# Eight idle bf16 matmuls at the start become five, followed by 64 matmuls on 32x32 tiles of the array

## The chip, the cores and the metric

The kernel runs on one core of one Trainium2 chip. The metric is the device time of one execution in microseconds. Three runs of the kernel before took 342.63, 343.73 and 343.97 us; the median is 343.73 us.

## The reference

The reference is block-causal attention over 8 batches and 8 heads (sequence 576, head size 64, blocks of 64), followed by a soft mixture of experts on its output, all in fp32:

```python
scores = scale * np.matmul(q, k.transpose(0, 1, 3, 2))      # q, k, v: (8, 8, 576, 64)
scores = np.where(block_i >= block_j, scores, -1e9)
attn = softmax(scores);  x = (attn @ v) laid out as (4608, 512)

logits = x @ phi                        # phi: (512, 32), 8 experts of 4 slots
d = softmax(logits, axis=0)             # over all 4608 rows
slot_input = d.T @ x                    # (32, 512)
slot_out[e] = relu(slot_input[e] @ w1[e]) @ w2[e]   # w1, w2: 16 MB each
c = softmax(logits, axis=1)
out = c @ slot_out                      # (4608, 512)
```

Softmax subtracts the maximum and adds 1e-9 to the sum. The matmuls that the change touches compute nothing of this.

## The kernel before

The attention stage goes through 32 pairs of heads. For each pair it loads q, k and v (SP issues the DMAs), scales k on POOL (`scale_k`, line 426), computes the scores on PE (`qk`, line 462, and `qkb`, line 483), finds row maxima on DVE (`rowmax`, lines 496 and 501), takes exponentials on ACT (line 511), normalises on POOL, transposes the probabilities on PE (line 549) and multiplies with v (lines 581 and 591). After each batch of four pairs come the logits (lines 609 and 616) and the running sums of the expert inputs. All these steps of all pairs are put in one list, each with a due time from a table written out by hand, and are emitted sorted by that time (`at`, and the loop at line 859); on each engine they run in that order, and `tc.manual_schedule` leaves the order as it is.

After the attention stage the experts follow: `up` (line 961), `down` (line 981), and the output `emit` (line 936), with the weights arriving by DMA in 32 pieces of 1 MB.

A PSUM tile `ps_all` of 128 partitions by 4096 fp32 columns is all eight banks; `bank` picks 512 columns of it. `idle` is a 128x64 bf16 tile of zeros, set by DVE at line 281. `acc` is a 128x512 fp32 tile, zeroed by POOL at line 289, in which the expert inputs are summed up much later.

Because `warm` is given the due times -50, -49.99 and so on, its matmuls are the first that PE executes. They multiply zeros by zeros: 128 rows by 64 columns of the array, 512 moving columns, into the bank `pb`, and nothing reads the result. PE's first real work comes behind them in its queue: the scores of the first pair, `qk` with "5" (two fp32 calls with 384 columns, one on rows 0 to 63 of the array, one on rows 64 to 127), which need q and the scaled k. DVE's first pass over scores (line 496) needs these.

An fp32 call of `nc.tensor.matmul` appears in the trace as two pairs of a weight load (LDWEIGHTS) and a MATMUL.

`tile_position=(r, c)` puts a matmul on the part of the array that begins at row r and column c; the size of the part is that of its operands. Line 609 uses four parts of 128 rows by 32 columns, line 936 four of 32 rows by 128 columns, line 483 four of 64 by 64.

Of the kernel before, what the change touches and what calls it, by code (L numbers as in the profile page):

```python
# [18 lines left out]
NS = 32  # L19
# [18 lines left out]
NPB = 2  # L38
ONE = "3"
NXT = 6  # L40
WARM = 8
RES = 17

XIN = (2, 3)
# [209 lines left out]
def tile_attention_softmoe(  # L254
# [9 lines left out]
    nc = tc.nc  # L264
# [9 lines left out]
    for qd in range(2):  # L274
        for g in range(4):
            r = slice(NS * g, NS * (g + 1))
# [3 lines left out]
    idle = const.tile([128, 64], BF16, name="idle")  # L280
# [4 lines left out]
    acc = const.tile([128, DM], F32, name="acc")  # L285
# [50 lines left out]
    with ExitStack() as c1:  # L336
# [3 lines left out]
        ps_all = ps.tile([128, 4096], F32, name="ps")  # L340

        def bank(k, i=0, z=""):
            n = BK.get(k + z, BK.get(k))[i]
            return ps_all[:, 512 * n:512 * n + 512]
# [53 lines left out]
        def at(t, fn, *args):  # L398
            ops.append((t, len(ops), fn, args))

        probs, xTs, xps = {}, {}, {}
# [28 lines left out]
        def warm(i):  # L430
            if i == 0:
                xps["w"] = bank("pb", 0, ".0")
            nc.tensor.matmul(  # L433
                xps["w"][0:64], lhsT=idle, rhs=idle[:, 0:64].unsqueeze(1).broadcast_to([128, 8, 64]), start=True, stop=True
            )


        def fill(bank, n):
# [362 lines left out]

        for i in range(WARM):
            at(-50 + 0.01 * i, warm, i)
# [58 lines left out]
    with ExitStack() as c2:  # L862
        start = c2.enter_context(ExitStack())
# [190 lines left out]
```

## Time and profile before

| | |
|---|---|
| median of three runs | 343.73 us (342.63 to 343.97) |
| profiled execution | 344.26 us, its span 342.2 us |
| PE busy | 330.0 us (96%), 5664 matmuls |
| DVE, ACT, POOL busy | 272.6, 257.5, 206.6 us |
| granted clock of PE, mean | 0.988 |

The span goes from the first to the last instruction; the execution's time has some 2 us more around it. Engines are PE (matrix), PEld (its weight loads, which overlap with PE), DVE, ACT, POOL and SP (which issues the DMAs). Times are microseconds from the span's start. A matmul's duration in the trace contains its latency; durations of matmuls side by side overlap, so start times are the better guide to throughput.

### The profile page before, as it was taken

Reading aid. Unit: us, or ns where it says so; the run is one execution under the profiler, and the core shown is the slowest. Engines: PE = TensorE matmul, PEld = TensorE weight load, DVE = VectorE, ACT = ScalarE, POOL = GpSimd, SP = SyncE. Lnnn points to the kernel's source line nnn. Section 1 sums busy time; section 2 is a strip of 40 time slices with the busy share of each in tenths; the row PEclk is TensorE's granted clock in tenths of the full one; section 3 lists DMA queues with packets and bytes.
Section 4 is the critical chain, followed back from the end, with each engine's and each line's share of the span. In section 5 each row is a group of like instructions: output and inputs, shape, how many; then the busy total and the mean of one; then the engine's idle time right before and its main releaser. Section 6 shows DMA issues by size and latency. Waiting matters only on the chain.

```text
span 342.2 us, 14342 instructions
## 1 busy us (share of the span) xinstructions
PE 330.0 (96%) x5664; PEld 231.3 (68%) x5664; DVE 272.6 (80%) x821; ACT 257.5 (75%) x850; POOL 206.6 (60%) x475
## 2 busy tenths in 40 slices
PE   8899999999999999999999999999999998999991
PEld 4567767767866786678667866786677875256660
DVE  5987888899889998998889988988898766373442
ACT  3998999889988898889888988898889823222332
POOL 3888794769577957695769576957777832100000
PEclk9999999999999999999999999999999999899997
DMA  5756629535643585356445863664322299999887
GB/s 180 249 166 215 229 73 318 174 92 208 216 146 98 213 300 179 100 212 212 132 114 214 297 178 92 226 215 157 106 72 71 51 365 402 362 424 406 356 324 306
DMA packets 29938, 72.28 MB, mean 211 GB/s; under 512 B 6960, under 2 KB 15280, under 8 KB 25776
## 3 DMA queue, kind: packets, MB, share of 16 engines
q1 hardware_dynamic: 29872, 71.38, 60.3%
q8 instruction: 44, 0.72, 0.8%
q14 instruction: 22, 0.18, 0.2%
HBM read 61.93 MB, written 9.44 MB: 209 GB/s over the span
## 4 chain that ended last, share of the span: by engine, by line
PE 93%; DVE 4%; issue 1%; DVEq 0%; ACT 0%
PE ps L581 22%; PE ps L549 16%; PE ps L462 15%; PE ps L483 11%; PE ps L591 6%; PE hp L961 5%; PE so L981 4%; PE o L936 3%; PE ps L718 3%; PE ps L609 2%; PE ps L738 2%; DVE ps L496 1%; PE ps L616 1%; PE ps L433 1%; DVE stat L501 1%; PE ps L747 1%
## 5 line engine op out<-in xcount | busy, mean ns | idle before, releaser
L511 ACT ACTIVATE arena<-ps,stat 128x384 f32<-128x384 f32 (+6 forms) x288 | 152.9, 543 | 25.3 <-DVE stat L496 21.9
L529 POOL TENSOR_SCALAR arena<-arena,stat 128x512 f32<-128x512 f32 (+6 forms) x288 | 152.8, 550 | 16.6 <-DVE stat L518 13.1
L496 DVE CUSTOM_DVE_ANT_1 ps<-ps,mask 128x384 f32<-128x384 f32 (+1 forms) x128 | 77.7, 635 | 7.4 <-PE ps L462 6.3
L394 DVE COPY arena<-ps 128x384 f32<-128x384 f32 (+3 forms) x134 | 68.4, 555 | 9.9 <-PE ps L549 3.8
L581 PE MATMUL ps<-arena 128*64 128x256 f32 (+2 forms) x640 | 76.1, 384 | 0.0
L392 ACT COPY arena<-ps 128x384 f32<-128x384 f32 (+3 forms) x142 | 65.2, 495 | 11.0 <-PE ps L549 7.6
L501 DVE TENSOR_REDUCE stat<-ps 128x1 f32<-128x64 f32 (+4 forms) x160 | 57.9, 402 | 6.1 <-ACT arena L511 3.7
L581 PEld LDWEIGHTS ps<-arena 128*64 128x64 f32 x640 | 40.9, 137 | 31.7 <-issue 18.8
L549 PE MATMUL ps<-ident,arena 64*128 64x64 f32 x1600 | 61.0, 226 | 1.0 <-ACT arena L511 0.8
L462 PE MATMUL ps<-arena 64*128 64x384 f32 (+1 forms) x256 | 61.1, 567 | 0.6 <-ACT arena L511 0.6
L549 PEld LDWEIGHTS ps<-ident,arena 64*128 64x128 f32 x1600 | 56.2, 139 | 4.8 <-ACT arena L511 0.9
L511 ACT ACTIVATION_READ_ACCUMULATOR arena<-ps,stat 128x1 f32 x288 | 59.4, 206 | 0.0
L483 PEld LDWEIGHTS ps<-arena 64*64 64x64 f32 x768 | 36.5, 133 | 21.2 <-ACT arena L392 4.6
L522 POOL TENSOR_SCALAR stat<-stat 128x2 f32<-128x2 f32 (+1 forms) x96 | 19.0, 198 | 47.4 <-ACT arena L511 41.4
L483 PE MATMUL ps<-arena 64*64 64x288 f32 (+4 forms) x768 | 42.9, 341 | 0.0
L462 PEld LDWEIGHTS ps<-arena 64*128 64x128 f32 x256 | 24.3, 189 | 10.1 <-DVE arena L394 4.0
L426 POOL TENSOR_SCALAR arena<-arena 128x576 f32<-128x576 f32 x32 | 21.6, 676 | 6.1 <-DMA arena<-in_k 4.6
L591 PE MATMUL ps<-arena 128*64 128x64 f32 x640 | 24.3, 222 | 0.0
L591 PEld LDWEIGHTS ps<-arena 128*64 128x64 f32 x640 | 22.6, 138 | 0.4
L394 DVE COPY xT<-ps 128x512 f32<-128x512 f32 (+1 forms) x27 | 15.2, 580 | 9.1 <-PE ps L581 8.8
L946 DVE COPY arena<-o 128x512 f32<-128x512 f32 (+1 forms) x20 | 11.7, 632 | 13.1 <-PE o L936 13.0
L496 DVE DVE_READ_ACCUMULATOR2_ANT stat<- 128x1 f32 x128 | 17.9, 140 | 0.0
(116 smaller groups left out, 286.2 us busy)
## 6 DMA issues: line engine op xcount, KB each, us to landing
arena<-in_w SPq DMA_DIRECT2D x32, 1024.0 KB, 7.1
arena<-in_k SPq DMA_DIRECT2D x32, 288.0 KB, 3.0
arena<-in_q SPq DMA_DIRECT2D x32, 288.0 KB, 3.2
out<-arena SPq DMA_DIRECT2D x18, 512.0 KB, 4.2
arena<-in_v SPq DMA_DIRECT2D x32, 256.0 KB, 3.4
arena<-in_v SPq DMA_DIRECT2D x32, 32.0 KB, 3.5
arena<-in_phi SPq DMA_DIRECT2D x1, 64.0 KB, 3.9
```

Source lines behind the costliest of these rows:

```text
L392: nc.scalar.copy(out=out, in_=in_)
L394: nc.vector.tensor_copy(out=out, in_=in_)
L426: nc.gpsimd.tensor_scalar(out=area(f"ks{m % NQB}"), in0=area(f"ks{m % NQB}"), scalar1=SCALE, scalar2=0.0, op0=ALU.mult, op1=ALU.add)
L462: nc.tensor.matmul(scores(t + str(j), m), lhsT=q[r, lo:lo + 128], rhs=k[r, 0:NC[t]], start=True, stop=True)
L483: nc.tensor.matmul(o, lhsT=a, rhs=b, start=True, stop=True)
L496: nc.vector.tensor_tensor_reduce(out=sc, in0=sc, in1=ms, scale=-1.0, scalar=-NEG, op0=ALU.add, op1=ALU.min, accum_out=st[:, 0, u:u + 1],)
L501: nc.vector.tensor_reduce(out=st[:, 0, u:u + 1], in_=scores(x, m), axis=AX.XY if x == "8" else AX.X, op=ALU.max, negate=True)
L511: nc.scalar.activation(out=pr, in_=sc, func=AF.Exp, bias=st[:, 0, u:u + 1], accum_out=st[:, 1, u:u + 1], scale=-1.0 if x[0] in "75" else 1.0,)
L529: nc.gpsimd.tensor_scalar(out=pr, in0=pr, scalar1=st[:, 2, u:u + 1], scalar2=0.0, op0=ALU.mult, op1=ALU.add)
L549: nc.tensor.transpose(out=trbank(m, g)[i][:, 64 * n:64 * n + 64], in_=prob(m, x)[r, 128 * c:128 * c + 128], identity=ident[r, r],)
L581: nc.tensor.matmul(xps[m, 0][64 * j:64 * j + 64, lo:hi], lhsT=vs(m)[:, j, c, :], rhs=rhs, start=n == 0, stop=n == 4, skip_group_check=True,)
L591: nc.tensor.matmul(xps[m, 1][64 * j:64 * j + 64, 0:64], lhsT=vs(m)[:, j, c, :], rhs=arena[:, lo:lo + 64], start=(c == 0), stop=(c == NQ - 1),)
```

## The change

`WARM` goes from 8 to 9. Calls 0 to 4 of `warm` stay as they are. Each of the calls 5 to 8 issues 16 matmuls instead: for each of four row groups j and four column groups c of the array, a 32x32 weight tile from `acc`, 128 moving columns from `acc` (rows of group j), with the result in partitions 32c to 32c+31 of the first 128 columns of bank j. `acc` still holds its zeros, and nothing reads the results.

```diff
-WARM = 8
+WARM = 9
...
         def warm(i):
             if i == 0:
                 xps["w"] = bank("pb", 0, ".0")
-            nc.tensor.matmul(
-                xps["w"][0:64], lhsT=idle, rhs=idle[:, 0:64].unsqueeze(1).broadcast_to([128, 8, 64]), start=True, stop=True
-            )
+            if i < 5:
+                nc.tensor.matmul(
+                    xps["w"][0:64], lhsT=idle, rhs=idle[:, 0:64].unsqueeze(1).broadcast_to([128, 8, 64]), start=True, stop=True
+                )
+                return
+            for j in range(4):
+                for c in range(4):
+                    r = slice(NS * j, NS * (j + 1))
+                    nc.tensor.matmul(
+                        ps_all[NS * c:NS * (c + 1), 512 * j:512 * j + 128], lhsT=acc[r, 0:NS], rhs=acc[r, 128:256],
+                        start=True, stop=True, tile_position=(NS * j, NS * c),
+                    )
```

(`NS` is 32.)

## Rows read from the trace of the kernel before

**Rows 1.** The page: span, busy time by engine, instruction queue.
```profile
span 342.2 us, 14342 instructions
PE 330.0 (96%) x5664; PEld 231.3 (68%) x5664; DVE 272.6 (80%) x821; ACT 257.5 (75%) x850; POOL 206.6 (60%) x475
...
PEclk9999999999999999999999999999999999899997
...
q8 instruction: 44, 0.72, 0.8%
```

**Rows 2.** The chain of waits, 0 to 30 us: start, us, what.
```profile
0.95 3.62 PE ps L433 x8
4.57 1.63 PE ps L462 x4
6.21 0.55 DVE ps L496
...
14.59 0.81 DVE arena L394 x2
15.39 0.04 issue
15.44 1.17 PE ps L549 x27
```

**Rows 3.** Busy time by stage: stretch, length, engines (instructions), clock, DMA, GB/s.
```profile
6.20:15.40 9.20, 7.68 (x83) 5.10 (x83) 9.16 (x32) 8.43 (x31) 7.12 (x23) 1.00 0.67 210
15.40:280.00 264.60, 264.56 (x4660) 194.07 (x4662) 231.58 (x708) 229.75 (x776) 194.12 (x438) 1.00 0.54 175
280.00:289.50 9.50, 8.01 (x169) 5.89 (x166) 6.73 (x22) 2.92 (x12) 1.06 (x4) 1.00 0.99 389
289.50:293.10 3.60, 3.60 (x17) 0.79 (x17) 1.54 (x4) 0.68 (x1) 1.16 (x1) 0.53 1.04 376
```

**Rows 4.** Instructions in order of time, 0 to 14 us: start, us, instruction.
```profile
0.87 0.53 POOL L289 MEMSET acc<- 128x512 f32 x1
...
0.95 3.62 PE L433 MATMUL ps<-idle 128*64 128x512 bf16 x8 [0.95 <-DVE zrun L292]
...
3.58 0.67 POOL L426 TENSOR_SCALAR arena<-arena 128x576 f32<-128x576 f32 x1 [1.70 <-DMA arena<-in_k]
...
4.50 0.51 PEld L462 LDWEIGHTS ps<-arena 64*128 64x128 f32 x4 [0.81 <-POOL arena L426]
```

**Rows 5.** Lines 433, 462 (4 to 6.2), 483 (first four; 6 to 7.4): ns min/median/max.
```profile
L433 PE MATMUL ps<-idle x8: 634/634/636, 1.0 to 3.9; 128*64 128x512 bf16 x8
...
L462 PE MATMUL ps<-arena x4: 844/925/1007, 4.5 to 5.3; 64*128 64x384 f32 x4
...
L483 PE MATMUL ps<-arena x4: 451/522/541, 6.1 to 6.1; 64*64 64x288 f32 x2, 64*64 64x256 f32 x1, 64*64 64x192 f32 x1
...
L483 PE MATMUL ps<-arena x24: 216/376/541, 6.1 to 7.3; 64*64 64x288 f32 x8, 64*64 64x256 f32 x4, 64*64 64x192 f32 x4, 64*64 64x128 f32 x4
```

**Rows 6.** PE's matmuls in order of time, 6.05 to 6.12 us.
```profile
5.30 0.85 PE L462 MATMUL ps<-arena 64*128 64x384 f32 x2
6.09 0.55 PE L483 MATMUL ps<-arena 64*64 64x288 f32 x4
```

**Rows 7.** Line 609, 56.4 to 57.7 us: order of time (one narrow window), then durations.
```profile
56.52 0.32 PE L609 MATMUL ps<-xT,arena 128*32 128x128 f32 x4
...
56.52 0.64 PE L609 MATMUL ps<-xT,arena 128*32 128x128 f32 x16
56.98 0.62 PE L609 MATMUL ps<-arena 128*32 128x128 f32 x16
...
L609 PE MATMUL ps<-xT,arena x16: 272/273/297, 56.5 to 56.9; 128*32 128x128 f32 x16
```

**Rows 8.** Line 936, 310.82 to 310.85 us: order of time, then durations.
```profile
310.83 0.71 PE L936 MATMUL o<-cT,s 32*128 32x512 f32 x4
...
L936 PE MATMUL o<-cT,s x4: 692/692/692, 310.8 to 310.8; 32*128 32x512 f32 x4
```

**Rows 9.** The chain of waits, 262 to 343 us: start, us, what.
```profile
263.32 1.01 PE ps L609 x32
264.33 0.45 PE ps L616 x32
...
289.49 3.58 PE hp L961 x16
293.07 0.31 PE z_ps L877 x2
293.38 12.15 PE hp L961 x112
```

## The prediction

> **What bounds the kernel now.** I went from the page to the chain of waits, then to the stages, then to the first microseconds line by line. The page has PE busy 330.0 of 342.2 us [rows 1]; the reader should see that this average hides two stretches without full PE. The chain of the first 30 us shows the first: it goes through the eight idle matmuls (0.95 to 4.57), through the first four score matmuls of line 462 (to 6.20), and then stays on DVE until 15.39, from where PE carries it [rows 2]. The stages say the same by busy time: DVE 9.16 of 9.20 us between 6.20 and 15.40, then PE 264.56 of 264.60 us up to 280 [rows 3]. So whatever makes the first scores late pushes a full DVE, which pushes a full PE, and I take such a delay to reach the end one for one. From 280 on DVE chains, the clock (0.53 granted between 289.5 and 293.1) and PE share the time [rows 3]; all of it follows the attention stage and shifts with it.
>
> The change sits ahead of all this. The idle matmuls are cover for the wait on the first k: POOL starts scaling it at 3.58, when its DMA is in, takes 674 ns (to 4.25), and PE's first score weight load is released by that at 4.50 [rows 4]. Eight idle matmuls of 512 columns start 427 ns apart ((3.62 - 0.634) / 7), that is 1.2 columns per ns, the 1.2 GHz level, and the last has streamed at 0.95 + 8 x 0.427 = 4.37 [rows 4, 5]. They end just as k is ready. The page's clock row shows 9 for these slices; I go by the durations. The clock rises while the first group of line 483 runs: its first four passes take 451 to 541 ns, and later ones of the same shapes are shorter (median 376 over the stage) [rows 5]. I set the rise at 6.3, an estimate between their start at 6.09 and their end.
>
> **The change part by part.**
>
> *Removed:* three idle matmuls, 3 x 0.427 = 1.28 us of PE. Alone this would gain nothing, because the first score load waits for POOL until 4.50 anyway.
>
> *Added:* 64 calls. An fp32 call is two instruction pairs of load and matmul: line 609 has 16 calls to a batch (four chunks by four groups) and 32 matmuls in the trace [rows 9]. So 128 loads and 128 matmuls. A matmul of 128 fp32 columns takes two cycles a column: line 609's first sixteen, four at a time, start at 56.52 and its next sixteen at 56.98, so a step takes (0.46 - 0.025) / 4 = 0.109 us at the 2.4 GHz level (256 cycles; the 0.025 is the first weight load, below) [rows 7]; at 1.2 GHz 256 cycles are 0.213 us.
>
> No row has 32x32 tiles, so how many run at once must be bounded. One at a time costs 128 x 0.213 = 27.3 us at 1.2 GHz; sixteen at once is 8 steps x 0.213 = 1.71 us. The nearest rows each show four tiles side by side: four column tiles (line 609: four starts span 0.32 - 0.297 = 0.02 us, 7 ns apart), four row tiles (line 936: 0.71 us for four of 0.692) and two by two (line 483: 0.55 us for four of up to 0.541) [rows 5 to 8]. Reads of sixteen tiles are four streams to a partition, as in line 609; writes are four row groups to four banks, as in line 936. Both are shown at full speed, so I take sixteen at once. Issue fits: 16 x 7 ns = 0.11 us a step, under 0.213.
>
> The Trainium skill has a rule against this: "TensorE: Matmul & The Clock Gate", in the section "Wait — 56ns, not 53.3ns?", says that matmuls never start closer than about 25 ns. By it the added part would take 128 x 25 ns = 3.2 us. The trace disagrees for tiles beside each other: line 616's 32 matmuls take 0.45 us of the chain, 14 ns each [rows 9].
>
> *The sum.* Five idle matmuls stream until 0.95 + 5 x 0.427 = 3.09. A change of tile form costs 0.14 us: the second passes of line 462 start at 5.30 and stream 384 x 2 / 1.2 = 0.64 us, to 5.94, and the new form starts at 6.09 [rows 6]. So the rounds start at 3.23. The first weight load adds 0.05 (297 against 272 ns in line 609, twice that at half clock [rows 7]), the eight steps 1.71, the staggered starts 15 x 7 ns = 0.10: end 5.09. Another change of form: the first score load starts at 5.23 instead of 4.50. Its first pass waits 0.16 for weights as now (1.007 against 0.844 us [rows 5]), to 5.39; two passes of 0.64 would end at 6.67, but from 6.3 the clock is double, which halves the last 0.37: end 6.48. Now they end at 5.94. **The first scores come 0.53 us late**; the matmuls after them lose nothing, since more of them run at 2.4 GHz.
>
> *What hides in this:* acc, which the new matmuls read, is zeroed by POOL from 0.87 for 0.53 us, long before 3.23 [rows 4]. The banks that they write are PE's own at that time, in order. The 256 instructions are about one more instruction packet (44 packets for some 11,500 PE instructions); such a packet takes 0.8% x 16 x 342.2 / 44 = 1.0 us of a DMA engine [rows 1]. I cost it at nothing, as it is fetched ahead behind the slow idle matmuls; uncovered it is at most 1.0 us.
>
> The profiled execution takes 344.26 us, a 342.2 us span and 2.1 around it, and is 0.53 above the median of the runs. On its own time the sum is 344.26 + 0.53 = 344.79; on the median 343.73 + 0.53 = 344.3. The runs before spread over 1.3 us, more than the effect. Under 0.5% (1.7 us) I count as no change.
>
> **The rivals.**
>
> *A start floor, or eight tiles at once.* With 3.2 us for the rounds they end near 6.5, the scores start at 6.6 and, all at the 2.4 level (0.1 for weights, then 2 x 0.32), end at 7.35: 1.4 late, 345.1. For it: sixteen tiles with two passes each need PE to look past far more waiting instructions than the rows with four show. Against it: the 14 ns of line 616.
>
> *Four at once (slower).* If PE gets no further ahead than in the rows, the rounds are 32 steps: 6.83 us at 1.2 GHz. 3.03 pass before 6.3, the other 3.80 take 1.90; end 8.2, scores start 8.34, end 9.08: 3.1 late, **346.9**. It decides as soon as the scores end 1.7 late, at 7.67: the rounds would then last until 6.8, which by the same arithmetic is about seven tiles at once. For it: nothing beyond four is shown. Against it: row and column tiles each reach four, and line 483 combines them.
>
> *The clock rises sooner.* The idle matmuls use 64 of 128 columns; full-array rounds might bring the 2.4 GHz level earlier. At best it rises at 3.23: the rounds take 8 x 0.11, the scores start at 4.50 behind POOL and end at 5.24 instead of 5.94: 0.7 gained, 343.0. Against it: in the profile PE was busy without a gap from 0.95 and the level still stayed at 1.2 GHz past 6.09, and the first 3 us are unchanged.
>
> *The late clock dip moves.* Line 961's first 16 matmuls take 3.58 us of the chain, where 16 of the next 112 take 12.15 / 7 = 1.74 [rows 9]: 1.84 us for a dip that starts at 289.6, beside a stretch of PE gaps. If the shift moved it off that work, 344.3 - 1.8 = 342.4. That the dip depends on when the program starts is likely, so this is mostly spread, not effect.
>
> **How the numbers follow.** Sixteen at once 0.57 (344.3, own range 343.2 to 345.2), floor or eight 0.15 (345.1), four or fewer 0.12 (346.9 and more), earlier clock 0.10 (343.0), dip moved 0.06 (342.4). The prediction is 344.3. The range 342.9 to 345.9 leaves out the four-at-once case and the moved dip, some 2 in 10. Slower by over 0.5% (above 345.45): four or fewer, a third of the floor case and a tail of the first, 0.20. Faster (below 342.0): only dip and clock together, 0.05. Within: 0.75.
>
> **What would show it.** Line 433 keeps 427 ns for five matmuls. The new line has 128 matmuls, with sixteen starts inside 0.12 us and about 1.9 us in all; the gaps on either side are 0.14. The first load of line 462 starts at about 5.2, the first DVE pass of line 496 at about 6.7 instead of 6.19, and PE takes over the chain at about 15.9 instead of 15.44. Starts of 25 ns or more apart, or steps in groups of four, show the slower rivals; score passes of 0.32 us spacing before 5.5 the earlier clock. The forecast is wrong in kind if the DVE stretch absorbs the delay, so that PE takes over at 15.4 as before.

## The result, and the profile after

The changed kernel took 344.61 us (median of 12 runs, 343.88 to 347.9); the kernel before, in the same series, 343.49 (12 runs, 341.81 to 345.4). The ratio is 1.0052, interval 1.0029 to 1.0075: slower by 1.1 us on the medians, and by 1.8 (1.0 to 2.6) by the ratio, right at the bound of 0.5% between "no change" and "slower". The ratios here and below are formed over the runs of a series and not from the two medians, and leave out one run of e4 that fell in a slower state. The prediction was 344.3 us, range 342.9 to 345.9.

The two profiled executions hardly differ (span 342.1 against 342.2 us), but not because nothing changed: two delays in the one and a clock dip in the other happen to be of like size. First the page of the changed kernel, against [rows 1].

```profile
span 342.1 us, 14592 instructions
...
PE 329.2 (96%) x5789; PEld 232.2 (68%) x5789; DVE 272.6 (80%) x821; ACT 257.5 (75%) x850; POOL 206.6 (60%) x475
...
PEclk9999999999999999999999999999999999999996
```

There are 250 more instructions (256 for the rounds, less three pairs), 45 instruction packets instead of 44, and no 8 in the clock row where the kernel before has one near the end.

Next the changed kernel's first 8 us in order of time (start, us, instruction), against [rows 4, 6]. The change shifts the line numbers: the idle matmuls are line 434, the new rounds 441, the scores 471 and 492 (462 and 483 before), DVE's pass 505 (496).

```profile
0.95 2.34 PE L434 MATMUL ps<-idle 128*64 128x512 bf16 x5 [0.95 <-DVE zrun L292]
3.22 2.59 PE L441 MATMUL ps<-acc 32*32 32x128 f32 x128
5.75 0.92 PE L471 MATMUL ps<-arena 64*128 64x384 f32 x4
6.59 1.32 PE L492 MATMUL ps<-arena 64*64 64x288 f32 x24
...
6.69 0.57 DVE L505 CUSTOM_DVE_ANT_1 ps<-ps,mask 128x384 f32<-128x384 f32 x1 [2.25 <-PE ps L471]
```

The rounds start at 3.22, as computed, but the scores follow at 5.75 and not at 5.23. The scores then need 0.92 us instead of 1.65, because the clock has risen already. The same kernel's chain of waits for the first 30 us shows the net effect, against [rows 2].

```profile
5.82 0.90 PE ps L471 x4
6.71 0.55 DVE ps L505
...
15.94 1.17 PE ps L558 x27
```

DVE starts at 6.71 (6.21 before), PE takes over at 15.94 (15.44 before): 0.50 us late at both. Line 590 (line 581 before) opens one group of matmuls per pair of heads; its groups start 0.49 to 0.53 late for the first 21 pairs, and 1.40 late for the 22nd. What happened between them is in the chain of waits around 196 us, first of the changed kernel:

```profile
193.50 0.91 PE ps L471 x4
...
195.67 0.45 PE ps L625 x32
196.11 0.23 PE ps L727 x2
196.35 0.72 issue
197.06 1.16 PE ps L727 x29
198.22 0.70 PE ps L471 x4
```

and the same place in the kernel before (618, 625 and 727 are 609, 616 and 718 there):

```profile
195.18 0.50 PE ps L616 x32
195.68 1.15 PE ps L718 x30
196.82 0.70 PE ps L462 x4
```

PE stops for 0.72 us in the middle of line 727, with nothing to wait for that the profile shows. I read this as PE having run out of instructions; e3, below, shows such a stop beside the transfer of a packet. The next line starts at 198.22 instead of 196.82, 1.40 late. Another 0.19 is regained before the expert stage, where the chain of the changed kernel reads, against [rows 9]:

```profile
290.70 1.92 PE hp L970 x16
...
292.93 12.15 PE hp L970 x112
```

It begins at 290.70 (289.49 before), 1.21 late, but these sixteen matmuls take 1.92 us instead of 3.58: the profiled execution of before had a clock dip here (0.53 granted from 289.5 to 293.1, [rows 3]), and this one has none. So 1.21 lost minus 1.66 gained leaves line 970's remaining 112 matmuls 0.45 earlier; at the end of the span only 0.1 of this is left. The dip is not an effect of the change: of the full kernels below e3, e9 and e10 show it in their profiles, the others don't.

### The profile page after: what moved, and what is told of

Read it like the earlier page. It is cut to its first block, busy times and chain, and to the rows that moved or that the text cites. A ratio compares the mean times of both kernels' runs of the same rounds, so it can differ in the third digit from the quotient of the medians.

```text
span 342.1 us, 14592 instructions
## 1 busy us (share of the span) xinstructions
PE 329.2 (96%) x5789; PEld 232.2 (68%) x5789; DVE 272.6 (80%) x821; ACT 257.5 (75%) x850; POOL 206.6 (60%) x475
## 4 chain that ended last, share of the span: by engine, by line
PE 94%; DVE 2%; ACT 1%; issue 1%; DVEq 0%
PE ps L590 22%; PE ps L558 17%; PE ps L471 15%; PE ps L492 12%; PE ps L600 6%; PE so L990 4%; PE hp L970 4%; PE o L945 3%; PE ps L727 3%; PE ps L618 2%; PE ps L747 2%; PE ps L625 1%; ACT arena L520 1%; PE ps L441 1%; PE ps L756 1%
## 5 line engine op out<-in xcount | busy, mean ns | idle before, releaser
L471 PE MATMUL ps<-arena 64*128 64x384 f32 (+1 forms) x256 | 60.4, 561 | 0.5 <-ACT arena L520 0.5
```

The costliest lines, as they stand in the source:

```text
L471: nc.tensor.matmul(scores(t + str(j), m), lhsT=q[r, lo:lo + 128], rhs=k[r, 0:NC[t]], start=True, stop=True)
```

## The experiments

Two questions: does the delay of the first scores explain the result, and why did the rounds take longer than computed? Theory A (late scores) is that the first scores' delay alone is what the end sees. Its rivals are that the rounds or their form move the rise of the clock, and, once the hole at 196 us had been seen, theory B (packets): the shifted count of PE's instructions opens holes in the dense part of the attention stage. In the profile's terms, the first rise is the first clock record of a trace; ahead of it durations are at the 1.2 GHz level. Diffs are against the changed kernel unless they say otherwise, and each ratio is to the kernel before, run in the same series.

**e1: the five idle matmuls alone, no rounds.**

```diff
-WARM = 9
+WARM = 5
```

> Five idle matmuls and no 32x32 matmuls at all. Late-scores theory (the loss is the time by which the rounds hold back the first score matmul): idle work ends at 3.09, the first score load starts at 4.50 behind POOL as in the kernel before, the first DVE score pass starts at 6.2; the time is that of the kernel before within 0.2%. Clock rival (the work ahead of the scores sets when the 2.4 GHz level comes): 1.4 us without PE work, so the level comes later than the 5.4 to 6.3 us of the two profiles, the scores and the first line of 64x64 matmuls run at 1.2 GHz, first DVE pass still near 6.2, but PE takes over the chain more than 1 us after 15.4 and the time rises by 1 to 2 us.

Measured: 346.39 us (7 runs) against 343.07; 1.0086 [1.0046, 1.0127]. Its first scores in order of time, and then its chain of waits at 198 us:

```profile
4.56 1.65 PE L471 MATMUL ps<-arena 64*128 64x384 f32 x4 [1.26 <-POOL arena L426]
6.14 2.41 PE L492 MATMUL ps<-arena 64*64 64x288 f32 x24
```
```profile
198.74 0.99 issue
199.74 1.15 PE ps L727 x28
```

The scores start on time, but behind 1.26 us of idle PE the clock rose only at 9.63, line 492 took 2.41 us instead of 1.40, and PE took over at 16.65. So cover of some sort is needed: leaving it out costs at least as much as the change (the two intervals overlap). And the hole is here too, where no rounds ever ran; its count of PE instructions is 6 fewer than before.

**e2: two rounds.**

```diff
-WARM = 9
+WARM = 7
```

> Five idle matmuls and two rounds of 16 instead of four. Late-scores theory: in the profile of the changed kernel a round takes 0.43 us when it is the first and 0.66 us after that at 1.2 GHz, so two end near 4.4 and the first score load starts at 4.5 to 4.7; time that of the kernel before plus 0 to 0.2 us. Rival (any 32x32 round costs a fixed amount, by a change of the array's form): first score load no earlier than 5.2 and most of the changed kernel's loss stays.

Measured: 345.39 against 343.07; 1.0065 [1.0038, 1.0092]. Its chain of waits at two places:

```profile
127.00 0.92 PE ps L727 x24
127.92 0.85 issue
...
309.80 1.11 issue
```

The first scores are no longer late (first matmul at 4.68, DVE at 6.13, PE takes over at 15.39), and still the kernel loses as much. Theory A alone is refuted. With 122 more PE instructions than before, there are holes of 0.85 and 1.11 us, at other places.

**e3: eight rounds.**

```diff
-WARM = 9
+WARM = 13
```

> Five idle matmuls and eight rounds of 16 instead of four. Late-scores theory: four more rounds of 0.41 us (2.4 GHz level) to 0.66 us (1.2) delay the first score load by 1.6 to 2.6 us against the changed kernel's 5.75, to 7.4 to 8.4; the score matmuls then all run at 2.4 GHz, so DVE starts at 8.3 to 9.3, and the time is 2 to 3 us above the kernel before. Rival (the delay is absorbed before PE takes over, and the measured difference is the spread of the clock): time within 0.5 us of the changed kernel's.

Measured: 351.61 (6 runs) against 343.07; 1.024 [1.0194, 1.0287], some 8 us above the kernel before, where I had expected 2 to 3. Its chain of waits, 3 to 10 us:

```profile
3.29 4.31 PE ps L441 x214
7.60 1.55 issue
9.15 0.84 PE ps L441 x34
```

The rounds ran dry for 1.55 us in their own middle, at 7.60, while a packet of the instruction queue was in transfer from 6.75 to 7.70. The clock, up at 6.85, fell at 10.26 behind this stop and rose again at 13.67; PE took over at 21.48. So an uncovered packet cost 1.55 us here, not the "at most 1.0" of the prediction.

**e4: the same rounds in bf16**, one pass instead of two.

```diff
-    lhsT=acc[r, 0:NS], rhs=acc[r, 128:256],
+    lhsT=idle[r, 0:NS], rhs=idle[r, 0:64].unsqueeze(1).broadcast_to([NS, 2, 64]),
```

> Four rounds of 16 as in the change, but on bf16 zeros, so that each call is one load and one matmul instead of two of each. Window theory (the hole between rounds comes from PE holding only so many instructions at a time, about one fp32 round): 32 instructions a round fit twice, so the rounds follow without a hole, 0.11 us each at 1.2 GHz or as fast as instructions are issued (16 pairs at 7 to 9 ns: 0.11 to 0.15), end by 3.9, first score load at 4.50, time that of the kernel before within 0.2%. Rival (each new round of calls waits for the last to drain, whatever its type): a hole of about 0.2 us after each round stays, end near 4.5, first score load at 4.5 to 4.8.

Measured: 345.79 (11 runs) against 343.07; 1.0072 [1.0043, 1.0102]. In order of time:

```profile
3.23 0.85 PE L441 MATMUL ps<-idle 32*32 32x128 bf16 x64
4.53 1.65 PE L471 MATMUL ps<-arena 64*128 64x384 f32 x4 [0.46 <-POOL arena L426]
6.11 2.41 PE L492 MATMUL ps<-arena 64*64 64x288 f32 x24
```

The scores start on time, but with 0.46 us of idle PE ahead of them the clock rose at 8.52, PE took over at 16.37, and there is a hole of 1.11 at 310.4. (At 203.8 PE waits 0.26 us for POOL, behind a k whose DMA took 6.28 us; that is no hole of this kind.) Again no gain from scores that start on time. What this kernel shows of the rounds' own duration is taken up in the next section.

**e5: the count alone, 6 fewer instructions.** The idle time of before in other pieces, no 32x32 tiles: one bf16 idle matmul and two fp32 calls of 448 columns, together as long as eight.

```diff
-WARM = 9
+WARM = 3
...
-            if i < 5:
+            if i == 0:
...
+            else:
+                nc.tensor.matmul(xps["w"][0:64, 0:448], lhsT=acc[:, 0:64], rhs=acc[:, 0:448], start=True, stop=True)
```

> The kernel before with PE's program six instructions shorter and the idle stretch equally long: one bf16 idle matmul and two fp32 ones of 448 columns (0.43 + 2 x 1.49 = 3.41 us at 1.2 GHz) instead of eight bf16 ones. Packet theory (PE's instructions come in packets of 256; the changed kernel has 250 more, that is six fewer up to whole packets, and the packet ends then fall where PE needs instructions fastest): first score load at 4.5 and first DVE pass near 6.2 as in the kernel before, but a PE hole of 0.4 to 1.0 us that waits for nothing shown, among the transposes of line 718 near 196 us, as in the three kernels with 250, -6 and 506 more instructions; PE's later stages 0.5 to 1.0 us late, time 0.1 to 0.4% above the kernel before. Late-scores theory alone: no hole, time that of the kernel before within 0.2%.

**e6: the changed kernel with 6 more instructions**, three short idle matmuls ahead of the rounds, which makes 256 more than before, exactly one packet.

```diff
+            if i == 5:
+                for _ in range(3):
+                    nc.tensor.matmul(xps["w"][0:64, 0:64], lhsT=idle, rhs=idle, start=True, stop=True)
```

> The changed kernel with three idle matmuls of 64 columns ahead of the rounds, so that PE's program is 256 instructions longer than the kernel before, one whole packet. Packet theory: the rounds still hold the scores back (first score load 5.8 to 6.1, PE takes the chain over 0.6 to 1.4 us after 15.4), but no hole near 196 us and none at any other place of the attention stage that the kernel before does not have; the delay at 16 us is the delay at 280 us within 0.2; time 0.2 to 0.45% above the kernel before, and less than the changed kernel's by 0.5 to 0.9 us. Rival (the hole belongs to something that the rounds do, the banks or acc, not to the count): hole near 196 stays, time as the changed kernel's.

**e7: the changed kernel again**, with no edit, beside these two.

> The changed kernel once more, on the chip of the two runs beside it. Packet theory: again a hole of 0.4 to 1.0 us among the transposes of line 727 (718 in the kernel before) near 196 us. All theories: the rounds again 0.43 us for the first and 0.66 for each later one at 1.2 GHz; the clock's rise falls elsewhere than at 5.3, between 4.5 and 8.5, and with a later rise the first DVE pass is later than 6.71. Time 0.3 to 0.7% above the kernel before.

Measured, against 343.75 (29 runs): e5 344.04, 1.0012 [0.998, 1.0044]; e6 344.9, 1.0036 [1.0001, 1.0072]; e7 345.41, 1.0057 [1.0023, 1.0091]. The chains of waits near 197 us, of e5, e6 and e7 in this order:

```profile
197.43 0.23 PE ps L721 x2
197.66 0.77 issue
```
```profile
197.24 0.44 PE ps L628 x31
197.68 0.36 issue
```
```profile
196.00 0.24 PE ps L727 x2
196.24 0.95 issue
```

Minus six instructions opens the hole in the same line after the same two matmuls, with rounds (e7) or without (e5). With 256 more it is smaller and in another line; I had expected none there, so that was a miss, taken up under the instruction packet below. As a change of time, however, the hole alone (e5) is not resolved: its interval holds zero. In e5's profile the first scores were early as well, and a late load of a later pair's k (its DMA took 5.85 us, POOL waited 2.0) cost 1.8 us between 130 and 139 us.

**e8: before with 42 more instructions**, three of its eight idle matmuls cut into 24 short ones. **e9: the changed kernel with 42 more**, in the same way. Both shift the packets off the line at 196 us.

```diff
 # e8: calls 5 to 7 of the kernel before; e9: calls 2 to 4 of the changed one
+                for _ in range(8):
+                    nc.tensor.matmul(xps["w"][0:64, 0:64], lhsT=idle, rhs=idle, start=True, stop=True)
```

> The kernel before with three of its idle matmuls cut into 24 of 64 columns: the same 3.4 us of idle work, 42 more instructions. Packet theory: packet ends come 42 instructions earlier in the work, for the batch near 194 us among the transposes that lie ahead of it (about 192.3 in the times of the kernel before, against 193.1 there and 193.8 or later with six fewer); no hole among lines 609, 616 and 718 near 196 us; first scores as in the kernel before for the same rise of the clock; time within 0.3% of the kernel before. Rival (holes come and go with the DMA traffic, not with the count): holes of 0.3 us and more near 196 here as often as in the kernels with six fewer.

> The changed kernel with three of its five full idle matmuls cut into 24 of 64 columns: the same idle work and the same four rounds, 42 more instructions, which is 36 more than the kernel before up to whole packets. Packet theory: the rounds' delay of the scores stays (first score load 5.3 to 6.0 by the clock's rise, DVE 6.2 to 7.4), the hole near 196 us that the changed kernel showed twice (0.72 and 0.95 us) is gone; time 0.5 to 0.9 us under the changed kernel's median, 0.2 to 0.4% above the kernel before. Rival (the rounds themselves or the traffic make the hole): hole of 0.3 us and more near 196, time 0.5% above the kernel before.

Measured, against 343.21 (23 runs): e8 343.85, 1.0031 [0.9997, 1.0064]; e9 345.43, 1.006 [1.0028, 1.0092]. The chain of e8 at 59 us and at 196 us:

```profile
59.87 0.32 issue
...
196.21 1.17 PE ps L722 x32
```

The hole at 196 us is gone from both, as theory B has it, but a smaller one stands at 60 us (0.32 in e8, 0.20 in e9), and e9 is no faster than the changed kernel. I had expected 0.5 to 0.9 us; that was a miss. Removing the hole in the profile did not show in the timed runs.

**e10: the rounds early**: one idle matmul, seven short ones, then the rounds, so that they end as k arrives. **e11: e6 once more**, beside it.

```diff
 # e10
-            if i < 5:
+            if i < 1:
...
+            if i < 5:
+                for _ in range(7 if i == 4 else 0):
+                    nc.tensor.matmul(xps["w"][0:64, 0:64], lhsT=idle, rhs=idle, start=True, stop=True)
```

> One full idle matmul and seven of 64 columns instead of five full ones, then the four rounds: PE's program is 256 instructions (one packet) longer than that of the kernel before, and the rounds begin near 1.9 and end near 4.5, where the idle matmuls of the kernel before end. Late-scores theory: first score load at 4.5 to 4.7, first DVE pass 5.5 to 6.3 by the clock's rise as in the kernels with idle matmuls alone, time that of the kernel before within 0.2%. Rival (rounds instead of idle matmuls move the clock's rise, or cost elsewhere): rise later than 7.5 us although PE is busy from 0.95 on, or a loss of over 0.3% although the scores are on time.

> The changed kernel with three idle matmuls of 64 columns ahead of the rounds, once more beside the run with early rounds: the same count of instructions, but rounds from 3.4 to about 6. Late-scores theory: first score load 5.4 to 6.2, time 0.3 to 0.5% above the kernel before and above the run with early rounds. Rival: the two runs agree.

Measured, against 342.81 (23 runs): e10 344.59, 1.005 [1.0019, 1.008]; e11 344.78, 1.004 [1.0015, 1.0065]. In order of time, e10 and then e11:

```profile
1.89 2.82 PE L445 MATMUL ps<-acc 32*32 32x128 f32 x128
4.64 1.65 PE L475 MATMUL ps<-arena 64*128 64x384 f32 x4
```
```profile
6.13 1.65 PE L474 MATMUL ps<-arena 64*128 64x384 f32 x4
7.71 2.41 PE L495 MATMUL ps<-arena 64*64 64x288 f32 x24
```

e10 has scores on time and no hole at 196 us, and is still 0.5% slower, where theory A wanted it within 0.2%; it also agrees with e11, whose scores are late. Its profile has a rise at 7.24 (6.30 before), POOL starting on the second pair's k at 8.06 (7.18 before) and PE taking over at 16.03, 0.59 late. In e11 the clock rose only at 10.17, though the profile shows PE busy without a break from 0.95 on; PE took over 2.5 us late. In e6, the very same program, the rise was at 7.10 and PE took over 1.33 late. One profile is one draw of the rise.

**e12: the rise by itself.** 42 bursts in one kernel, each behind a pause, in three forms.

```diff
+    for i in range(REPS):
+        for n, form in enumerate(((0, 0, 30), (5, 4, 19), (1, 4, 23))):   # idle, rounds, idle
+            pause(200 + (i * 3 + n) * 773 % 1800)
+            burst(*form)
```

> Nothing of the reference is computed: PE stays silent behind a chain of DVE copies and then works about 12 us on zeros, 42 times in turn in three forms: 30 idle matmuls; 5 idle matmuls, 4 rounds of 16 and 19 idle matmuls (the order of the changed kernel); 1 idle matmul, 4 rounds and 23 idle matmuls. Read is the time from a burst's first matmul to the rise of the clock. Theory that the rounds count for less than idle matmuls (two runs with rounds had the rise at 10.2 and 7.2 us although PE was busy from 0.95 on): the mean rise is later by 0.3 to 1.5 us with rounds behind five idle matmuls, and later still behind one, and single rises come after 7.5 us only in the forms with rounds. Rival (any work counts alike and the rise falls by chance): the three means agree within 0.3 us, all rises between 3 and 7 us after the start.

Two of its bursts, by the view of stretches (length, busy time and count of each engine, then granted clock): one of five idle matmuls and four rounds from 67.20, and one of one idle matmul and four rounds from 285.15.

```profile
67.20:72.80 5.60, 5.60 (x135) 3.17 (x136) 5.46 (x5) 0.00 (x0) 0.50 0.01 3
72.80:76.00 3.20, 3.20 (x17) 1.56 (x15) 3.10 (x4) 0.00 (x0) 0.99 0.00 0
285.10:291.30 6.20, 6.15 (x136) 3.50 (x137) 6.03 (x6) 0.00 (x0) 0.50 0.03 5
291.30:294.00 2.70, 2.70 (x14) 1.33 (x13) 2.63 (x3) 0.00 (x0) 1.00 0.00 0
```

The granted clock is 0.50, the 1.2 GHz level, for 5.6 and 6.2 us of full PE. Over 14 bursts each, the time from the first matmul to the rise was 4.40 us in the mean for idle matmuls alone (2.68 to 5.93), 4.45 for the change's order (2.90 to 5.80), and 5.00 for the early rounds (3.65 to 6.64). I had expected 0.3 to 1.5 us more for the change's order, and single rises after 7.5 us; neither came. Single bursts of a form scatter by about 1.0 us (standard deviation), so none of the differences between the means is resolved: the change's order is 0.06 us later (95% interval -0.7 to 0.9), early rounds 0.60 (-0.2 to 1.4). Both ends of the early rounds' spread lie later, which points to a delay but doesn't show one. The rise is spread over 3 us whatever the form.

## Why the prediction came out right, and where it was wrong

**The start of the rounds, and sixteen at once: right.** The changed kernel's rounds in narrow windows (order of time; the count shows how many have started by the window's end, 3.33, 3.55 and 3.68 us), then their durations:

```profile
3.22 0.52 PE L441 MATMUL ps<-acc 32*32 32x128 f32 x16
...
3.22 0.73 PE L441 MATMUL ps<-acc 32*32 32x128 f32 x32
...
3.22 0.84 PE L441 MATMUL ps<-acc 32*32 32x128 f32 x33
```
```profile
L441 PE MATMUL ps<-acc x32: 416/416/418, 3.2 to 3.5; 32*32 32x128 f32 x32
```

Sixteen start within 0.52 - 0.416 = 0.10 us, 7 ns apart, as forecast. The first round starts at 3.22 (3.23 forecast), so the idle step of 427 ns and the 0.14 us for a change of form hold. The rivals with four or eight tiles at a time fall. The Trainium skill's rule of about 25 ns between starts ("TensorE: Matmul & The Clock Gate", section "Wait — 56ns, not 53.3ns?"), cited in the prediction, does not hold for matmuls on different tiles: 7 ns here.

**The rounds' length: the term that was mis-sized.** I summed eight steps of 0.213 us, 1.71. The second sixteen do start 0.21 us after the first, but then nothing starts until the first matmul has ended, at 3.224 + 0.418 = 3.642; the 33rd starts at 3.668. From the 33rd on, a round takes 0.66 us at the 1.2 GHz level instead of 0.43: 67 have started by 4.36 and 101 by 5.02. That is a step of 0.213, a latency of 0.416 and some 0.03. In bf16 the limit sits at the same count, as e4's two windows to 3.52 and 3.54 us show:

```profile
3.23 0.44 PE L441 MATMUL ps<-idle 32*32 32x128 bf16 x32
...
3.23 0.57 PE L441 MATMUL ps<-idle 32*32 32x128 bf16 x33
```

There 32 matmuls start within 0.13 us, half the columns' work of the fp32 rounds, and the 33rd at 3.537, just after the first has ended (3.225 + 0.284 = 3.509). So it isn't columns or passes: no more than 32 matmuls, which with their weight loads are 64 instructions, are under way at once. The Trainium skill, "TensorE: Matmul & The Clock Gate", section "The mechanism", gives PE a reorder window 64 deep; 32 pairs of load and matmul are what such a window would hold, and the two traces agree with that depth (a limit of 32 matmuls would look the same). In the prediction I had the right worry, "PE to look past far more waiting instructions than the rows with four show", and put it on a rival with eight tiles; it strikes sixteen tiles as well, between rounds.

**The first scores 0.53 us late: right in number by two errors that cancel.** The rounds were longer by 0.52 (scores at 5.75, not 5.23), and the rise came at 5.30 instead of 6.3 in that execution, which halved what followed. In e7 the rise was at 3.88: scores at 5.29, DVE at 6.23, hardly later than the 6.19 of before. In e6 it was at 7.10: DVE at 7.54, 1.35 late (0.16 of it by the extra matmuls). So 0.5 is one draw from a spread, not a constant. Cover of the old length has such a spread too: DVE started at 6.19 for a rise at 6.30 (before), at 5.72 for 5.09 (e8), at 5.48 for 4.37 (e5). At like rise the change makes the first scores about 0.75 to 1.0 late: 6.23 at a rise of 3.88 against 5.48 at 4.37, and 6.69 at 5.30 against 5.72 at 5.09.

**One for one to the end: right for delays as far as the expert stage, not for gains.** In the changed kernel 0.50 at DVE is 0.50 at PE's takeover and stays until 196 us; e11's 2.53 at the takeover is still 2.49 at the last pair. What follows is not tested: from line 970's start to the end of the span the profiles without a dip or a hole there take 50.8 us (e1, e5, e7) to 52.3 (e8), a spread larger than the effect. But e8's DVE was 0.47 early and PE took over at 15.59, 0.15 late: POOL could start on the second pair's k only at 7.62 instead of 7.18, and that held the chain. An early rise is therefore only partly collected. That the DVE stretch would absorb the delay did not occur.

**"I cost it at nothing" for the instruction packet: wrong step.** The step looked at the start of the kernel alone. At the start the extra packet was indeed hidden, but 256 instructions less 6 shift every later packet boundary by six instructions against the program. In the changed kernel the packet near 194 us is in transfer at 194.74, behind line 471's slow stretch (0.91 us for four matmuls and their loads); before it was at 193.08, at the beginning of that stretch. What follows is the dense batch part, logits and transposes at 14 to 38 ns a matmul (32 in 0.45, 30 in 1.15 us), and there a packet moved in at 194.74 is late, one at 193.08 is not: the transfer starts 1.66 us later than before, but PE comes to the same count of instructions only 0.91 later (196.35 against 195.44). The difference, 0.75, is the stop of 0.72. The instruction queue from 193.0 to 193.3 us in the kernel before, then from 194.6 to 194.9 in the changed one (packets, MB, share of 16 engines):

```profile
q8 instruction: 1, 0.02, 19.6%
...
q8 instruction: 1, 0.02, 19.4%
```

The place follows the count: six fewer (in the count's remainder by 256) gave a hole between 196 and 203 us in all five profiles (0.72 and 0.95 changed, 0.99 e1, 0.77 e5, 0.38 e3); an unchanged remainder gave none in three of four (before, e10, e11; 0.36 in e6); 36 or 42 more moved it to 60 us; 122 more to 128 and 310 us, up to 1.11 us.

A count settles it, e6 included. Of all that the traces record for PE in order (matmuls, weight loads, semaphores, drains), the sixteen stops of over 0.1 us with nothing to wait for all begin when the number of records behind PE leaves 193 when divided by 256: 6849 in the changed kernel, e6 and e7, 6593 in e1 and e5, 7105 in e3, 1729 in e8. (Only the 0.45 us ahead of line 970, line 961 before, which every kernel has, doesn't fit.) So the ends of packets are fixed, 256 records apart, and the work moves past them; e6's stop is at the place of the others, six instructions earlier in the work. In all sixteen PE resumed 1.2 to 1.6 us after the end of the last packet's transfer. The kernel before passes this place 1.42 us after the transfer's end without a stop, e10 and e11 1.49 and 1.33, so with an unchanged remainder it is at the edge. That the stops lie at the ends of late packets is thereby shown; that they cost this much in every execution is not.

**The sum.** By the trace of the changed kernel 0.5 + 0.9 - 0.2 = 1.2 us at the expert stage; e7's profile has 1.33 there (290.82), with 0.03 of it from the start and the rest from a hole and two smaller stops. The timed medians are 1.1 and 1.7 us slower. So 344.3 was 0.3 us low, because only the first of two costs was in it, and the range held it. As a difference the forecast fits worse than as a time: 0.53 forecast, against 1.1 on the medians and 1.8 (1.0 to 2.6) by the ratio. The time came as close as it did also because the kernel before had 343.49 in this series, not 343.73; that is luck.

**The moved dip and the earlier clock.** The dip did go from the profiled execution, worth 1.66 us of the 1.84 forecast; this is spread, as I had said. The rise came before the scores ended in both profiles of the changed kernel, which the rival "the clock rises sooner" wanted, but in e12 the change's order came to 4.45 against 4.40 us, no difference that could be told from the spread.

**Open.** The timed runs don't split the loss: the shifted count alone is not resolved (e5 +0.12% [-0.2, 0.44], e8 +0.31% [-0.03, 0.64]), scores on time without the hole still lose 0.5% (e10), and moving the hole gave nothing back (e9). A later rise and late loads of k are in some of these profiles; whether they are in the timed executions can't be seen. No version beat the kernel before.

## What to carry to other kernels

Before packing many small tiles, count the instructions in flight: here 32 matmuls with their loads were the limit, so rounds of sixteen two-pass tiles ran in bursts with a latency of 0.42 us between them. An edit that adds or removes instructions anywhere on PE moves the instruction packets of everything after it; look for "issue" in the chain of waits where many short matmuls follow each other, and not at the edit alone. A profile is one execution: here its first clock rise (spread over 3 us) and one dip (1.7 us) were larger than the effect, and two equal spans hid 1.2 us.

## What the runs showed of the hardware that was not expected

Matmuls on sixteen 32x32 tiles start 7 ns apart, 32 of them before the first has ended, then none until it has. At the ends of instruction packets, 256 recorded instructions apart, PE stopped in some places for 0.14 to 1.55 us, without any wait in the profile, and went on 1.2 to 1.6 us after the last packet's transfer. The clock rose 2.7 to 6.6 us after the first matmul of a burst on an otherwise idle PE, and 9.2 us after it in e11 (0.95 to 10.17), with PE busy throughout.
